# Splitting V into two float16 parts on ScalarE and VectorE in an attention + MoE kernel, with a new table of due times

## The chip, the cores and the metric

The kernel runs on one core of one Trainium2 chip, as one program. The time is the device time of the whole program in microseconds (us). An engine's name in the profile is PE for TensorE's matmuls, PEld for its weight loads, DVE for VectorE, ACT for ScalarE, POOL for GpSimd and SP for SyncE, which here only starts DMAs.

## The reference, cut to what matters

Attention with rotary position embedding, for 4 batches x 8 heads, 576 tokens, 64 elements to a head:

```python
q_rot, k_rot = (rotate(q), rotate(k))
scores = scale * np.matmul(q_rot, k_rot.transpose(0, 1, 3, 2))
scores = scores - np.max(scores, axis=-1, keepdims=True)
attn = np.exp(scores)
attn = attn / (np.sum(attn, axis=-1, keepdims=True) + 1e-09)
return np.matmul(attn, v)
```

Its output, as 2304 tokens of 512 elements, goes through a mixture of 8 experts: gate probabilities P are normalised over rows and columns in turn eight times, and the output is the sum over e of P[:, e] * (relu(x @ w1[e]) @ w2[e]), with 1024 hidden elements.

## The kernel before, in words

**Two parts of a number.** TensorE multiplies float16 here wherever it can. A float32 operand is scaled by a power of two and split into a high part, which is its float16 rounding, and a low part, which is the float16 rounding of what is left. A product is then three matmuls: high x high, high x low, low x high. V, the softmax weights, x and the expert weights are all split so. The scores (line 406) are float32 matmuls.

**Attention.** The 32 heads are worked as 16 pairs, two heads side by side on the 128 partitions. For a pair, GpSimd turns q and k (rope: four multiplications, line 357, and two additions, line 361), and TensorE makes five score groups of four matmul instructions each (S, line 406; the profile has eight records to a group, 640 for the 80 groups). Each row block of scores is a tile of PSUM, of which three stand at a time. Per tile: VectorE takes the row maximum (line 410), ScalarE the exponential (line 417), VectorE the reciprocal of the sum (lines 423 and 425), ScalarE writes the scaled high part (line 428), VectorE the low part (line 292). In four tiles of nine the exponential is written to an SBUF tile `e`, and the scores' PSUM tile is free from there on; in the other five it stays in PSUM tile `s` until the low part is made. SyncE then starts a transposing DMA of the two parts (lines 458 and 462) into ET. Once a half pair's transposes have landed, TensorE multiplies them with V's parts (AV, line 477), and ScalarE and VectorE split the result into `xx` (lines 487 and 489).

**V.** A batch's V is loaded in four pieces of 128x640 (line 318). VectorE takes the largest magnitude of each (line 289), then of the four (line 328); TensorE turns that column into a row and spreads the result back to all partitions (lines 660 and 667; the same helper serves the gate's weights and expert 0's weights), and VectorE makes a power of two of it (lines 279 to 285). Before the change, for each of the 16 pairs: GpSimd multiplies the piece by that power in place (`v_x`, line 384), ScalarE casts it to the high part (`v_hi`, line 379), and GpSimd subtracts (`v_lo`, line 388). Two tiles hold split V (NVV = 2).

**Expert 0 inside attention.** The weights of expert 0 are scaled and split in the same way, in place on GpSimd (`wz`, line 549), ScalarE (`wh`, line 545) and GpSimd (`wl`, line 553). As soon as x of a batch is there, TensorE may run expert 0's first product (F1, line 611) and, once the last of the second weight's low parts is there, its second (F2, line 630); the code asks for `wl.2.7`, the eighth and last `wl` of that weight. These matmuls fill TensorE between score groups. The gate's normalisation and experts 1 to 7 (line 1092, a seven-product scheme over half experts) follow.

**What sets the order.** Each engine runs its instructions in the order in which they were recorded. That order is made at build time by a list scheduler (`Plan.run`): every operation has an engine, a cost in us, a due time `at` and dependencies; at each step an idle engine takes the ready operation with the smallest due time. The due times of the attention part are `AT`, `AT_NEW` and the offsets `SH1`, one to a kind of operation: `S` scores, `M` maximum, `ex` exponential, `ei` reciprocal, `eh` and `el` high and low part, `TR` transposes, `AV`, `ld` and `ldv` loads, `cq sq aq` and `ck sk ak` rope of q and k, `vx vh vl` V's scaling, high and low part. `choice(...)` gives GpSimd alone here, because BOTH is False. `lock=True` tells the scheduler that a VectorE operation is not to be put beside a GpSimd operation.

Of the kernel before, what the change touches and what calls it, by code (L numbers as in the profile page):

```python
# [14 lines left out]
ALU = mybir.AluOpType  # L15
# [4 lines left out]
B, H, S, D = 4, 8, 576, 64  # L20
NT, DM, NE, DF = B * S, 512, 8, 1024
NPAIR = B * H // 2
KC = DM // P
# [39 lines left out]
    ld=-78.23, cq=-29.0, ck=-28.0, vx=-11.0, sq=-29.0, sk=-28.0, aq=-28.5, ak=-27.5, vh=-10.0, vl=-9.0, h0=4.69, l0=5.19,  # L63
    h1=9.69, l1=10.19, S=-20.0, M=-20.0, ex=-20.0, eh=-10.0, el=-10.0, TR=-10.0, AV=5.0, ei=-20.0,
)
AT_NEW = dict(ldv=-30.41, v0=-10.46, v1=-9.46, v2=-8.46, v3=-7.46, vg=-6.96, vr=-6.86, vp=-6.46)
AV_AT = ((3, 0, 0), (3, 0, 1), (4, 0, 2), (5, 0, 3), (6, 0, 4), (7, 1, 0), (8, 1, 1), (9, 1, 2), (10, 1, 3), (11, 1, 4))

SH1 = dict(
    cq=11.55, sq=11.55, aq=11.55, el=9.37, vh=-16.21, ld=10.14, M=-76.45, S=-26.64, eh=-9.66, ex=-20.25, ck=-11.34,  # L70
    sk=-11.34, ak=-11.34, ldv=-6.42, AV=-36.11, TR=10.32, vx=11.72, vl=-32.41, x0=1.13, h0=1.13, l0=1.13, x1=1.13,
    h1=1.13, l1=1.13, ei=-12.59,
)

US = dict(
# [147 lines left out]
def attention_moe(ctx, tc, qk, v, trigs, eye, wg, w1, w2, out):  # L223
# [67 lines left out]
    def stt_lo(lo, x, s, hi):  # L291
        dve.scalar_tensor_tensor(lo, x, s, hi, op0=ALU.mult, op1=ALU.subtract)  # L292

    def hi_of(hi, x, s, e="act"):
        if e == "act":
            act.activation(hi, x, AF.Copy, scale=s)
        else:
            dve.tensor_scalar(hi, x, s, None, op0=ALU.mult)
# [76 lines left out]
    def v_hi(p):  # L375
        t = att.tile([P, 2, 640], F16, tag="vv", bufs=NVV, name="vv")
        vhl[p] = [t[:, n].rearrange("p (j a d) -> p j a d", j=2, a=5) for n in range(2)]
        b, c = divmod(p, KC)
        act.copy(vhl[p][0], vraw[b][:, c])

    def v_x(p, e):
        b, c = divmod(p, KC)
        x = vraw[b][:, c].rearrange("p j a d -> p (j a d)")
        engine[e].tensor_scalar(x, x, vs[b], None, op0=ALU.mult)

    def v_lo(p, e):
        b, c = divmod(p, KC)
        engine[e].tensor_tensor(vhl[p][1], vraw[b][:, c], vhl[p][0], op=ALU.subtract)

    HEADS = [slice(0, 64), slice(64, P)]  # L390
    QH = [slice(0, HS), slice(HS, S)]
# [258 lines left out]
    def choice(pool_us, dve_us):  # L650
        return (("pool", US[pool_us]), ("none", 0.0))[:1] + ((("dve", US[dve_us]),) if BOTH else ())
# [25 lines left out]
    def pair_ops(p):  # L677
# [4 lines left out]
        def add(k, e, us, fn, deps=(), **kw):  # L682
            e = e if isinstance(e, tuple) else (e, US[us])
            plan.add(f"{k}.{p}", e, at[k], fn, [d if "." in d else f"{d}.{p}" for d in deps], **kw)
# [11 lines left out]
        for i in range(5):  # L696
# [14 lines left out]
            for j in range(1 if i == TAIL else 2):  # L711
# [19 lines left out]
                    f"TR.{m}", ("sp", US["TR"]), at["TR"] + u + off(u), lambda m=m: e_turn(m), [f"el.{m}"] + [f"et{h}.{p}" for h in hs],  # L731
                    uses=[e] + [(f"ET{h}", p) for h in hs], allocs=tails if u == 4 else [],
                )
        add("vx", choice("tsv", "tsd"), 0, lambda e: v_x(p, e), [f"vp.{b}"], uses=[("vraw", b)])
        add("vh", "act", "vh", lambda: v_hi(p), ["vx"], allocs=[("vhl", p)], uses=[("vraw", b)])
        add("vl", choice("plv", "tt"), 0, lambda e: v_lo(p, e), ["vh"], uses=[("vraw", b), ("vhl", p)])
        done = None
        for s, qh, jt in AV_AT:
            a, et = ("G", ("av", p, qh)), (f"ET{qh}", p)
# [63 lines left out]
    def w0_ops():  # L803
        plan.add("gx", ("dve", 0.3), 8, gate_max)
        last, g = top_ops("g", 8, "gx", lambda: w0m["g"])
        plan.add("gs", ("dve", 1.0), 8, gate_scale, [last], uses=[g], lock=True)
        for n, at in ((1, 16.95), (2, 66.94)):
            r = ("raw0", n)
            for i in range(4):
                plan.add(  # L810
                    f"w.{n}.{i}", ("sp", 5.5), at - 30 + 2 * i, lambda n=n, i=i: w0_load(n, i), [f"w.{n}.{i - 1}"] if i else [],
                    allocs=[] if i else [r], uses=[r] if i else [],
                )
                plan.add(f"wm.{n}.{i}", ("dve", US["w"]), at + i, lambda n=n, i=i: w0_max(n, i), [f"w.{n}.{i}"] + ([f"wm.{n}.{i - 1}"] if i else []), uses=[r])
            plan.add(f"wx.{n}", ("dve", 0.25), at + 4, lambda n=n: w0_max1(n), [f"wm.{n}.3"])
            last, g = top_ops(f"w{n}", at + 4, f"wx.{n}", lambda n=n: w0m[n])
            plan.add(f"ws.{n}", ("dve", 0.7), at + 5, lambda n=n: w0_scale(n), [last], uses=[g], lock=True)
            for i in range(8):
                d = [f"wz.{n}.{i - 1}"] if i else []
                plan.add(f"wz.{n}.{i}", choice("tsw", "tsd"), at + 5 + 3 * i, lambda e, n=n, i=i: w0_x(n, i, e), [f"ws.{n}"] + d, uses=[r])  # L820
                d = [f"wh.{n}.{i - 1}"] if i else []
                plan.add(f"wh.{n}.{i}", ("act", US["wh"]), at + 6 + 3 * i, lambda n=n, i=i: w0_hi(n, i), [f"wz.{n}.{i}"] + d, uses=[r])
                d = [f"wl.{n}.{i - 1}"] if i else []
                plan.add(f"wl.{n}.{i}", choice("plw", "wl"), at + 7 + 3 * i, lambda e, n=n, i=i: w0_lo(n, i, e), [f"wh.{n}.{i}"] + d, uses=[r])
        plan.add("acc", ("none", 0.0), 0, open_acc, ["wl.2.7"])
# [598 lines left out]
```

## Time and profile before

| | us |
|---|---|
| median of 3 runs | 1685.58 |
| lowest and highest run | 1684.28, 1691.61 |
| the profiled execution's own time | 1691.59 |
| its span, first to last instruction | 1689.6 |
| last attention matmul (line 477) starts | 425.7 |
| engines' busy share of the span: PE, DVE, ACT, POOL | 94%, 82%, 62%, 36% |

The profiled execution is near the slowest of the runs shown, 6.0 us above the median, of which 2.0 us lie outside the span. Attention takes the first quarter of the span, and the change lies in that quarter alone; the mean shares of the whole say little about it. The page's 40 slices (42.2 us each) show a PE that fills up only from the sixth slice on, and a granted clock below full in the slices before.

### The profile page before, as it was taken

The page shows a single profiled execution, that of the slowest core. Times are in us where ns is not written, and L with a number is a line of the kernel's source. Part 1 is how long each engine was busy: PE and PEld are TensorE (multiplying, and loading weights), DVE is VectorE, ACT ScalarE, POOL GpSimd, SP SyncE. Part 2 cuts the span into 40 slices and gives each one's busy share as a digit, 9 for nine tenths or more (in the row PEclk, how much of TensorE's full clock was granted, in tenths as well). Part 3 has the DMA queues.
Part 4 walks back from the last instruction along what each step waited for, and adds up shares of the span by engine and source line. Part 5 has one row for each costly group of instructions (what it writes and reads, how often), then busy time and mean ns, then how long its engine had stood idle before and what let it go on. Part 6 is the DMA issues. An engine that isn't in the chain of part 4 may idle for free.

```text
span 1689.6 us, 35290 instructions
## 1 busy us (share of the span) xinstructions
PE 1583.7 (94%) x13990; PEld 1274.3 (75%) x13990; DVE 1377.7 (82%) x2736; ACT 1054.4 (62%) x2145; POOL 616.1 (36%) x504
## 2 busy tenths in 40 slices
PE   3676889999998999999999999999999999999998
PEld 2343445445456898989989898989898989898987
DVE  7667977877797888888888888888888878888877
ACT  3565766656237666666666666666666666666642
POOL 4767774620252423232323323232323323333310
PEclk9767988999999999999999999999999999999999
DMA  7899989977122565656555565655555555565532
GB/s 215 176 184 189 213 177 188 190 155 125 54 88 100 125 151 125 151 132 157 125 151 136 140 138 143 157 131 146 138 151 138 143 133 155 126 161 130 127 111 94
DMA packets 244853, 243.61 MB, mean 144 GB/s; under 512 B 195792, under 2 KB 195920, under 8 KB 241104
## 3 DMA queue, kind: packets, MB, share of 16 engines
q1 hardware_dynamic: 225968, 180.02, 39.5%
q0 software_dynamic: 18720, 61.35, 20.3%
q8 instruction: 109, 1.79, 0.4%
q14 instruction: 56, 0.46, 0.1%
HBM read 123.36 MB, written 9.44 MB: 79 GB/s over the span
## 4 chain that ended last, share of the span: by engine, by line
PE 79%; DVE 8%; DMA 3%; ACT 2%; issue 2%; SPq 0%; POOLq 0%; ACTq 0%; DVEq 0%
PE m L1092 66%; PE s L406 4%; PE g L477 4%; DMA ET<-et 3%; PE g L630 3%; PE g L611 2%; DVE et L292 2%; DVE nm L410 1%; DVE hl L621 1%; DVE ts L912 0%; ACT accA L879 0%; ACT et L428 0%; ACT e L417 0%; DVE w1l L292 0%; DVE ei L425 0%
## 5 line engine op out<-in xcount | busy, mean ns | idle before, releaser
L1092 PE MATMUL m<-w2h,h 128*128 128x256 f16 x3528 | 627.2, 273 | 3.2 <-DVE accB L1155 1.5
L1092 PEld LDWEIGHTS <-h 128*128 128x128 f16 x5292 | 515.3, 98 | 63.5 <-issue 2.0
L1092 PE MATMUL m<-w2l,h 128*128 128x256 f16 x1764 | 480.8, 273 | 0.0
L1092 PEld LDWEIGHTS <-w1h 128*128 128x128 f16 x3920 | 369.2, 98 | 39.9 <-issue 3.0
L1092 PE MATMUL m<-ts,w1h 128*128 128x256 f16 (+1 forms) x2240 | 347.6, 262 | 2.7 <-ACT m L1115 1.4
L1157 ACT ACTIVATE ev<-m,pp 128x256 f32<-128x256 f32 x468 | 197.6, 467 | 185.8 <-PE m L1092 184.8
L1092 PE MATMUL m<-ts,w1l 128*128 128x256 f16 (+1 forms) x1120 | 284.0, 262 | 0.0
L1092 PE MATMUL m<-xx,w1h 128*128 128x256 f16 (+1 forms) x1680 | 261.4, 262 | 0.0
L1042 POOL TENSOR_TENSOR wraw<-wraw 128x512 f32<-128x512 f32 x112 | 160.8, 1436 | 169.3 <-issue 140.6
L1092 PE MATMUL m<-xx,w1l 128*128 128x256 f16 (+1 forms) x840 | 213.1, 262 | 0.0
L1137 POOL TENSOR_TENSOR h<-u,h 128x512 f16<-128x512 f32 (+1 forms) x70 | 78.2, 1116 | 357.7 <-ACT h L1133 348.8
L1092 PEld LDWEIGHTS <-w1l 128*128 128x128 f16 x1960 | 191.8, 98 | 17.7
L1155 DVE SCALAR_TENSOR_TENSOR ev<-m,pp,ev 128x256 f32<-128x256 f32 x351 | 154.8, 478 | 45.4 <-ACT ev L1157 28.3
L406 PE MATMUL s<-raw 64*128 64x288 f32 (+1 forms) x640 | 136.7, 509 | 49.7 <-ACT e L417 19.5
L1133 ACT ACTIVATE h<-m 128x512 f16<-128x512 f32 (+1 forms) x210 | 120.4, 574 | 44.4 <-PE m L1092 40.8
L406 PEld LDWEIGHTS s<-raw 64*128 64x128 f32 (+1 forms) x640 | 72.2, 211 | 99.8 <-issue 28.0
L410 DVE TENSOR_REDUCE nm<-s 128x1 f32<-128x576 f32 x144 | 103.6, 752 | 48.6 <-PE s L406 48.1
L1118 DVE TENSOR_TENSOR u<-m,u 128x512 f32<-128x512 f32 (+1 forms) x140 | 88.9, 635 | 54.9 <-PE m L1092 29.2
L1133 ACT ACTIVATE h<-u 128x512 f16<-128x512 f32 (+1 forms) x210 | 122.4, 586 | 14.8 <-DVE u L1144 11.1
L1115 ACT COPY u<-m 128x512 f32<-128x512 f32 (+1 forms) x140 | 75.8, 541 | 71.5 <-PE m L1092 70.4
L1165 POOL DMA_DIRECT2D accA<-ev x78 | 69.0, 1021 | 126.5 <-ACT ev L1157 108.4
L1165 POOL DMA_DIRECT2D accB<-ev x52 | 45.1, 867 | 181.7 <-ACT h L1133 111.0
(148 smaller groups left out, 2629.8 us busy)
## 6 DMA issues: line engine op xcount, KB each, us to landing
ts<-xd SPq DMA_DIRECT2D x110, 512.0 KB, 3.8
accA<-ev POOLq DMA_DIRECT2D x78, 512.0 KB, 6.1
wraw<-in_w SPq DMA_DIRECT2D x28, 1024.0 KB, 4.9
raw<-in_qk SPq DMA_DIRECT2D x32, 576.0 KB, 5.0
accB<-ev POOLq DMA_DIRECT2D x26, 512.0 KB, 7.1
ts<-xd SPq DMA_DIRECT2D x28, 256.0 KB, 2.9
accB<-ev POOLq DMA_DIRECT2D x26, 256.0 KB, 3.3
vraw<-in_v SPq DMA_DIRECT2D x16, 320.0 KB, 4.4
```

The costliest lines, as they stand in the source:

```text
L406: pe.matmul(o, q, x[r, 1, QH[kh]], start=True, stop=True)
L410: dve.tensor_reduce(b[0], ps[:, :, 0:HS], axis=AX.XY, op=ALU.max, negate=True)
L477: pe.matmul(po[r, m : m + e.shape[-1]], x[:, j, jt, :], e[:, j, 5 * n + jt, :], start=jt == i == 0 and x is vh and n == 0, stop=jt == 4 an ...
L1042: put(k, "pool", US["ptt"], lambda: pool.tensor_tensor(quad(o), quad(x), quad(y), op=op), deps, uses=[raw])
L1092: pe.matmul(live[bank][:, f_ * width : (f_ + 1) * width], step(x, i, f_), y[:, i], start=first and f_ == 0 and n == 0, stop=n == 5, skip_g ...
L1115: act.copy(live[n], live[src])
L1118: dve.tensor_tensor(live[n], live[x], live[n], **add)
L1133: act.activation(t[:, 0:cols], live[src], func)
L1137: engine[eng].tensor_tensor(l, live[src], h, **sub)
L1155: dve.scalar_tensor_tensor(o, x, s, o, op0=ALU.mult, op1=ALU.add)
L1157: act.activation(o, x, AF.Copy, scale=s)
L1165: pool.dma_start(out=accs(th * NT2 + t0_, nt), in_=ev[th][:, 0:nt], accum_op=ALU.add)
```

## The change

V's high part is now made from the raw piece by one ScalarE activation with the power of two as its scale, and its low part by one VectorE instruction, raw x scale - high (`stt_lo`). The multiplication in place on GpSimd is gone, and so is GpSimd's subtraction. The operation count of V goes from three to two per pair. The due times are a new set: `AT_NEW` for V's maximum and scale, all of `SH1`, and the due times of expert 0's two weights. The instructions of the gate's part and of experts 1 to 7 stand in the same order as before on every engine; VectorE's last 2039 instructions and TensorE's last 23493 are the same.

```diff
-AT_NEW = dict(ldv=-30.41, v0=-10.46, v1=-9.46, v2=-8.46, v3=-7.46, vg=-6.96, vr=-6.86, vp=-6.46)
+AT_NEW = dict(ldv=-30.41, v0=-12.6, v1=-11.6, v2=-10.6, v3=-9.6, vg=-9.1, vr=-9.0, vp=-8.6)
 SH1 = dict(
-    cq=11.55, sq=11.55, aq=11.55, el=9.37, vh=-16.21, ld=10.14, M=-76.45, S=-26.64, eh=-9.66, ex=-20.25, ck=-11.34,
+    cq=-15.86, sq=-15.86, aq=-15.86, el=6.56, vh=-15.55, ld=29.61, M=-83.32, S=-99.0, eh=-8.21, ex=-31.64, ck=-3.35,
...
-        act.copy(vhl[p][0], vraw[b][:, c])
-
-    def v_x(p, e):
-        b, c = divmod(p, KC)
-        x = vraw[b][:, c].rearrange("p j a d -> p (j a d)")
-        engine[e].tensor_scalar(x, x, vs[b], None, op0=ALU.mult)
+        hi_of(vhl[p][0], vraw[b][:, c], vs[b])
 
-    def v_lo(p, e):
+    def v_lo(p):
         b, c = divmod(p, KC)
-        engine[e].tensor_tensor(vhl[p][1], vraw[b][:, c], vhl[p][0], op=ALU.subtract)
+        stt_lo(vhl[p][1], vraw[b][:, c], vs[b], vhl[p][0])
...
-        add("vx", choice("tsv", "tsd"), 0, lambda e: v_x(p, e), [f"vp.{b}"], uses=[("vraw", b)])
-        add("vh", "act", "vh", lambda: v_hi(p), ["vx"], allocs=[("vhl", p)], uses=[("vraw", b)])
-        add("vl", choice("plv", "tt"), 0, lambda e: v_lo(p, e), ["vh"], uses=[("vraw", b), ("vhl", p)])
+        add("vh", "act", "vh", lambda: v_hi(p), [f"vp.{b}"], allocs=[("vhl", p)], uses=[("vraw", b)])
+        add("vl", "dve", "vl", lambda: v_lo(p), ["vh"], uses=[("vraw", b), ("vhl", p)], lock=True)
...
-        for n, at in ((1, 16.95), (2, 66.94)):
+        for n, at in ((1, 17.16), (2, 58.97)):
```

The functions that it calls stood there before:

```python
def stt_lo(lo, x, s, hi):
    dve.scalar_tensor_tensor(lo, x, s, hi, op0=ALU.mult, op1=ALU.subtract)

def hi_of(hi, x, s, e="act"):
    if e == "act":
        act.activation(hi, x, AF.Copy, scale=s)
```

In the changed kernel the lines from `v_hi` on stand five lines earlier and those after the pair's operations six. Three places show what the new due times do.

VectorE, early in the program, up to the maximum over batch 0's V (`vm1`); `vmx` is the maximum of a piece of V, `wmx` of a quarter of expert 0's first weight, `wgs` the split gate weights, `nm` the row maximum of scores. Before:

```order
L279 TENSOR_SCALAR e_285<-g_165 128x1
L283 TENSOR_SCALAR inv_287<-e_285 128x1
L285 RECIPROCAL s_289<-inv_287 128x1
L588 TENSOR_SCALAR wgs_94<-wgt_93,s_289 128x4x8
L589 SCALAR_TENSOR_TENSOR wgs_94<-wgt_93,s_289,wgs_94 128x4x8
L289 TENSOR_REDUCE wmx_213<-wraw_149 128x1
L289 TENSOR_REDUCE vmx_195<-vraw_142 128x1
L328 TENSOR_REDUCE vm1_299<-vmx_195 128x1
```

And now:

```order
L289 TENSOR_REDUCE wmx_211<-wraw_149 128x1
L405 TENSOR_REDUCE nm_267<-s_258 128x1
L405 TENSOR_REDUCE nm_270<-s_259 128x1
L289 TENSOR_REDUCE vmx_191<-vraw_142 128x1
L418 TENSOR_SCALAR et_280<-es_272 128x1
L420 RECIPROCAL ei_282<-et_280 128x1
L418 TENSOR_SCALAR et_284<-es_278 128x1
L420 RECIPROCAL ei_286<-et_284 128x1
L289 TENSOR_REDUCE wmx_211<-wraw_149 128x1
L289 TENSOR_REDUCE vmx_191<-vraw_142 128x1
L328 TENSOR_REDUCE vm1_297<-vmx_191 128x1
```

The gate weights' five small instructions no longer stand ahead of `vm1`; a third `wmx` does.

TensorE at the same moment: the two matmuls that spread V's maximum (L660 and L667 before, L655 and L662 now), between score groups. Before:

```order
L406 MATMUL s<-raw 128x288 x8
L660 LDWEIGHTS vm_299
L660 MATMUL g<-idt,vm_299 1x128
L667 LDWEIGHTS neg
L667 MATMUL g<-top_309,neg 128x1
L406 MATMUL s<-raw 128x288 x8
```

And now:

```order
L401 MATMUL s<-raw 128x288 x8
L655 LDWEIGHTS vm_297
L655 MATMUL g<-idt,vm_297 1x128
L401 MATMUL s<-raw 128x288 x4
L662 LDWEIGHTS neg
L662 MATMUL g<-top_311,neg 128x1
L401 MATMUL s<-raw 128x288 x4
```

The sixth score group has moved between the two, so that it no longer stands behind the second.

GpSimd, where expert 0's second weight is finished (`wraw` scaled, `wl` its low parts) beside the rope of two pairs. Before, `raw_1848` is pair 9's and `raw_2085` pair 10's:

```order
L549 TENSOR_SCALAR wraw_1285<-wraw_1285,s_1724 128x512
L357 TENSOR_TENSOR raw_1848<-raw_1848,trig_95 128x576
L357 TENSOR_TENSOR raw_1849<-raw_1849,trig_95 128x576
L361 TENSOR_TENSOR raw_1848<-raw_1848,raw_1849 128x576
L357 TENSOR_TENSOR raw_1848<-raw_1848,trigq_96 128x576
L357 TENSOR_TENSOR raw_1849<-raw_1849,trigq_96 128x576
L361 TENSOR_TENSOR raw_1848<-raw_1848,raw_1849 128x576
L553 TENSOR_TENSOR wl_1727<-wraw_1285,wh_1726 128x512 x3
L549 TENSOR_SCALAR wraw_1285<-wraw_1285,s_1724 128x512 x2
L553 TENSOR_TENSOR wl_1727<-wraw_1285,wh_1726 128x512 x2
L357 TENSOR_TENSOR raw_2085<-raw_2085,trig_95 128x576
```

And now, where `raw_2056` is pair 10's:

```order
L548 TENSOR_TENSOR wl_1794<-wraw_1041,wh_1793 128x512
L357 TENSOR_TENSOR raw_2056<-raw_2056,trigq_96 128x576
L357 TENSOR_TENSOR raw_2057<-raw_2057,trigq_96 128x576
L361 TENSOR_TENSOR raw_2056<-raw_2056,raw_2057 128x576
L357 TENSOR_TENSOR raw_2056<-raw_2056,trig_95 128x576
L357 TENSOR_TENSOR raw_2057<-raw_2057,trig_95 128x576
L361 TENSOR_TENSOR raw_2056<-raw_2056,raw_2057 128x576
L548 TENSOR_TENSOR wl_1794<-wraw_1041,wh_1793 128x512 x2
L544 TENSOR_SCALAR wraw_1041<-wraw_1041,s_1791 128x512 x2
L548 TENSOR_TENSOR wl_1794<-wraw_1041,wh_1793 128x512 x2
```

The last four `wl` now stand behind the rope of pair 10, one pair later than before. On TensorE the first F2 matmul stands behind 46 score groups instead of 41, the first F1 matmul behind 24 instead of 28. Counted at the end of score group 46, 135 matmuls of expert 0 stood ahead before and 96 now; at group 58, 222 and 231; at the last group, 438 and 432.

## Rows read from the trace of the kernel before

**Rows 1.** The page: busy time by engine, and the clock in 40 slices.

```profile
PE 1583.7 (94%) x13990; PEld 1274.3 (75%) x13990; DVE 1377.7 (82%) x2736; ACT 1054.4 (62%) x2145; POOL 616.1 (36%) x504
...
PEclk9767988999999999999999999999999999999999
```

**Rows 2.** Busy us by stretch (window, length, engines), then granted clock, DMA share, GB/s.

```profile
40.00:165.00 125.00, 84.56 (x527) 50.47 (x528) 89.54 (x200) 73.74 (x155) 92.11 (x62) 0.76 0.90 184
165.00:205.00 40.00, 36.26 (x250) 18.52 (x246) 35.40 (x79) 28.75 (x61) 26.43 (x19) 0.99 0.96 211
205.00:235.00 30.00, 20.44 (x114) 12.15 (x115) 22.40 (x49) 17.91 (x39) 25.37 (x18) 0.66 0.94 193
235.00:440.00 205.00, 192.80 (x1486) 102.87 (x1486) 154.24 (x348) 129.09 (x269) 78.28 (x56) 0.97 0.79 156
440.00:522.00 82.00, 77.10 (x410) 40.11 (x408) 74.98 (x141) 30.96 (x56) 35.17 (x24) 1.00 0.21 76
```

**Rows 3.** The page: the chain that ended last, shares of the span by line.

```profile
PE m L1092 66%; PE s L406 4%; PE g L477 4%; DMA ET<-et 3%; PE g L630 3%; PE g L611 2%; DVE et L292 2%; DVE nm L410 1%; DVE hl L621 1%; DVE ts L912 0%; ACT accA L879 0%; ACT et L428 0%; ACT e L417 0%; DVE w1l L292 0%; DVE ei L425 0%
```

**Rows 4.** The score matmuls alone, line 406, by stretch: PE, PEld, clock, DMA.

```profile
40.00:160.00 120.00, 47.87 (x184) 25.36 (x184) 0.76 0.89 182
160.00:240.00 80.00, 24.38 (x120) 12.55 (x120) 0.85 0.91 194
240.00:320.00 80.00, 25.48 (x144) 14.21 (x144) 0.94 1.00 203
320.00:400.00 80.00, 22.40 (x136) 11.60 (x136) 0.98 0.76 141
```

**Rows 5.** What TensorE waited for in 0 to 240 us: total us, times, longest.

```profile
PE s L406 <- ACT e L417: 17.8, 13, 2.9
PE g L477 <- DMA ET<-et: 17.3, 8, 5.4
PE s L406 <- DVE et L292: 13.3, 7, 4.9
PE g L660 <- DVE vm L328: 11.1, 2, 8.7
PE s L406 <- POOL vv L388: 1.8, 1, 1.8
```

**Rows 6.** Groups by form in 0 to 440 us: busy us, mean ns, idle before.

```profile
L292 DVE SCALAR_TENSOR_TENSOR et<-e,ei,et 128x576 f16<-128x576 f32 x64 | 66.1, 1032 | 0.9 <-ACT et L428 0.8
L292 DVE SCALAR_TENSOR_TENSOR et<-s,ei,et 128x576 f16<-128x576 f32 x80 | 64.6, 810 | 15.0 <-ACT et L428 14.7
L428 ACT ACTIVATE et<-e,ei 128x576 f16<-128x576 f32 x64 | 49.5, 773 | 6.6 <-issue 2.6 <-ACT s L417 1.2 <-ACT xx L487 0.6
L384 POOL TENSOR_SCALAR vraw<-vraw,s 128x640 f32<-128x640 f32 x16 | 31.5, 1975 | 2.0 <-DVE s L285 2.0
L388 POOL TENSOR_TENSOR vv<-vraw,vv 128x640 f16<-128x640 f32 x16 | 22.4, 1397 | 68.8 <-ACT vv L379 68.8
L379 ACT CAST vv<-vraw 128x640 f16<-128x640 f32 x16 | 11.6, 723 | 9.2 <-PE g L477 9.2
```

**Rows 7.** Line 292 in 0 to 440 us: shortest, median, longest ns; first and last start.

```profile
L292 DVE SCALAR_TENSOR_TENSOR et<-e,ei,et x64: 796/819/1982, 28.5 to 413.3; 128x576 f16<-128x576 f32 x64
```

**Rows 8.** The timeline of DVE and PE around 36 to 41 us: start, length, what.

```profile
36.01 1.45 DVE L589 SCALAR_TENSOR_TENSOR wgs<-wgt,s,wgs 128x32 f16<-128x32 f32 x1
37.38 1.21 DVE L289 TENSOR_REDUCE wmx<-wraw 128x1 f32<-128x1024 f32 x1
39.34 0.16 DVE L328 TENSOR_REDUCE vm<-vmx 128x1 bf16<-128x4 f32 x1
39.56 0.27 PE L660 MATMUL g<-idt,vm 128*1 128x128 bf16 x1 [8.72 <-DVE vm L328]
...
40.87 0.16 PE L667 MATMUL g<-top,neg 1*128 1x1 bf16 x1 [1.04 <-DMA ET<-et]
```

**Rows 9.** The timeline of POOL around 223 us, as the second weight's low parts end.

```profile
223.15 2.62 POOL L553 TENSOR_TENSOR wl<-wraw,wh 128x512 f16<-128x512 f32 x2 [4.40 <-ACT wh L545]
225.73 3.27 POOL L357 TENSOR_TENSOR raw<-raw,trig 128x576 f32<-128x576 f32 x2
...
235.02 1.40 POOL L361 TENSOR_TENSOR raw<-raw 128x576 f32<-128x576 f32 x1
```

**Rows 10.** The F2 matmuls alone, line 630, by stretch: PE, PEld, clock, DMA.

```profile
360.00:400.00 40.00, 14.81 (x63) 5.58 (x63) 1.00 0.71 128
```

More of the change, by code (lines that the diff above doesn't have):

```diff
@@ L65 @@
 )
-AT_NEW = dict(ldv=-30.41, v0=-10.46, v1=-9.46, v2=-8.46, v3=-7.46, vg=-6.96, vr=-6.86, vp=-6.46)
+AT_NEW = dict(ldv=-30.41, v0=-12.6, v1=-11.6, v2=-10.6, v3=-9.6, vg=-9.1, vr=-9.0, vp=-8.6)
 AV_AT = ((3, 0, 0), (3, 0, 1), (4, 0, 2), (5, 0, 3), (6, 0, 4), (7, 1, 0), (8, 1, 1), (9, 1, 2), (10, 1, 3), (11, 1, 4))
 SH1 = dict(
-    cq=11.55, sq=11.55, aq=11.55, el=9.37, vh=-16.21, ld=10.14, M=-76.45, S=-26.64, eh=-9.66, ex=-20.25, ck=-11.34,
-    sk=-11.34, ak=-11.34, ldv=-6.42, AV=-36.11, TR=10.32, vx=11.72, vl=-32.41, x0=1.13, h0=1.13, l0=1.13, x1=1.13,
-    h1=1.13, l1=1.13, ei=-12.59,
+    cq=-15.86, sq=-15.86, aq=-15.86, el=6.56, vh=-15.55, ld=29.61, M=-83.32, S=-99.0, eh=-8.21, ex=-31.64, ck=-3.35,
+    sk=-3.35, ak=-3.35, ldv=3.34, AV=-35.53, TR=50.6, vx=12.14, vl=-38.21, x0=-3.51, h0=-3.51, l0=-3.51, x1=-3.51,
+    h1=-3.51, l1=-3.51, ei=9.58,
 )
```

## The prediction

> **What bounds the kernel now.** The page comes first: PE is busy 94% of the span, and its clock falls below full only in the first slices [rows 1]. So I cut the span by stage [rows 2]. From 440 us on, and in all of experts 1 to 7, the change moves nothing; there the chain of waits is TensorE's own matmuls, 66% of it on line 1092 alone [rows 3]. From 235 to 440 us PE is busy 192.8 of 205 us at a clock of 0.97: TensorE bounds that stretch as well, because expert 0's matmuls fill it. Before 235 us nothing is full: in 40 to 165 us PE is busy 84.6 of 125 us at a mean clock of 0.76 (a mix of its two levels, 1.2 and 2.4 GHz), VectorE 89.5, ScalarE 73.7, GpSimd 92.1, the DMA engines 0.90 [rows 2]. That is a pipeline held by its latencies. Its pace is read from the score matmuls, eight records to a group [rows 4]: 184 records are 23 groups in 120 us, 5.2 us each; then 15 in 80 us, 5.3 each; then, with more of expert 0 between them, 18 in 80 us (4.4) and 17 in 80 us (4.7). What TensorE waits for up to 240 us is ScalarE's exponential 17.8 us, the transposing DMAs 17.3, VectorE's low parts 13.3, V's maximum 11.1 and GpSimd's V 1.8 [rows 5]. The question is what the change does to the first 235 us, and whether TensorE then has the same work left.
>
> **The change, part by part.** All terms are us on the path; negative is a gain.
>
> GpSimd's V work. 16 multiplications (31.5) and 16 subtractions (22.4) go, 53.9 us of GpSimd [rows 6], 24% of the 222.2 that it is busy from 40 to 440 us [rows 2]. Only what TensorE waited for counts: 1.8 [rows 5]. Term -1.8; from -1.8 to 0.
>
> ScalarE's high part. 16 casts of 723 ns become scaled activations. The scaled copy of 128x576 out of SBUF takes 773 ns [rows 6], so 859 ns for 640 columns: 16 x 0.136 = 2.2 us more. ScalarE is busy 59% of 40 to 165 us [rows 2], which hides it. Term 0; up to 2.2 without that cover.
>
> VectorE's low part. 16 new instructions, a form that the trace has from SBUF with 576 columns: shortest 796, longest 1982 ns [rows 7], mean 1032 [rows 6]. By columns (640 to 576) that is 0.88 to 2.2 us each; I take the mean, 1.15, the nearest row. Against it, the same instruction with its large operand in PSUM takes 810 ns [rows 6], so the 64 from SBUF spend 66.1 - 64 x 0.810 = 14.3 us in waits, which I put down to GpSimd; 24% less GpSimd work saves 3.4 of them. Eight of the 16 low parts fall ahead of 235 us, as eight pairs' V does before: 8 x 1.15 - 1.7 = 7.5 us more on VectorE there. The other eight lie beside a full TensorE. VectorE idles 28% of 40 to 165 us, and what stands behind a low part is a row maximum or a reciprocal, for which ScalarE's exponential and then the next score group wait. I take a third of it on the path: +2.5; from -1.7 (they fill idle time, the savings do not) to 7.5.
>
> For this price the row shows a median of 819 ns against a longest of 1982 [rows 7], so most of the 64 met nothing. The Trainium skill, "SBUF — State Buffer", section "Who interferes with whom", says that a VectorE instruction with two SBUF inputs and a GpSimd instruction that reads SBUF shut each other out for a whole instruction; the new low part has two such inputs and the old VectorE share of V had none. Were each of the first eight shut out for one GpSimd subtraction of 1.4 us [rows 6], that would be an estimate of 11.2 us of VectorE time instead of the 2.2 that the mean holds above the shortest, and the term +5.5 instead of +2.5.
>
> The first V maximum. TensorE stood 8.7 us for it, until 39.56, and began group 6 only behind the second matmul of that helper, at 40.97 [rows 8]. On VectorE the gate weights' last instruction goes from ahead of it (36.01 to 37.38: -1.4) and a third maximum over a weight comes in (37.38 to the next start, at most 1.21: +1.2); on TensorE group 6 now follows the first helper matmul at once (39.83 instead of about 41.0: -1.2). Term -1.4; from -2.6 to 0.
>
> Expert 0's second product. It may begin once the last `wl` is through, which was at 225.8 [rows 9], and that now stands behind the rope of pair 10, which ran from 225.73 until 236.4, one V multiplication among it [rows 9]. In order, the first F2 matmul comes five score groups later, and 39 matmuls that stood ahead of the end of group 46 stand behind it: at 14.81/63 = 0.235 us [rows 10] 9.2 us of TensorE work leave a stretch with idle TensorE for one that is 94% full. The 24 F1 matmuls that now stand four groups earlier go the other way, but they lay in latency-bound time before and still do. By group 58 the order has caught up (231 against 222), so part of the 39 goes into idle time of 235 to 280 us. I take half: +4.6; from 0 to 9.2.
>
> The rest of the new order. Half-pair products stand up to three score groups earlier, maxima and low parts change places everywhere. The order does not say what that is worth. It can touch the three waits of 17.8, 17.3 and 13.3, 48.4 us together [rows 5]: I bound it by a quarter of them either way, 12, and take a tenth as a gain, -5, since GpSimd's rope, which feeds the scores, now runs without V's work between.
>
> Sum: -1.8 + 0 + 2.5 - 1.4 + 4.6 - 5 = -1.1. On the profiled execution's own 1691.59 that is 1690.5; this execution lies 6.0 above the median of the runs, 1685.58, so the forecast for the median is 1684.5: no change.
>
> **The rivals.** 0.5% of the time is 8.4 us; that is about what a measurement of this kernel can tell from none.
>
> Faster: the first 235 us become denser. For it speak 48.4 us of waits that depend on order [rows 5], a TensorE that in 40 to 165 us is busy 68% at 0.76 of its clock, and a later pace of 4.4 to 4.7 us with the same softmax work per group [rows 4]. Against it: the DMA engines are at 0.89 to 1.00 from 40 to 320 us [rows 4]. If the 38 groups of 40 to 240 us go at 4.85 instead of 5.2 to 5.3, 38 x 0.4 = 15 us are won: 1670. Chance 0.28.
>
> Slower: TensorE runs dry before expert 0's second product. Between the end of the first F1 block and the first F2 matmul stand 13 score groups now. Before, the dry stretch of 205 to 235 us shows what that costs: PE busy 20.4 of 30 us at a clock of 0.66 [rows 2]. If groups 42 to 46 go at 5.3 instead of 4.4 (4.5 us) and the 39 matmuls find no idle TensorE later (9.2), 13.7 us are lost; with the other terms, which sum to -5.7 without this one, and the reordering's -5 not coming, 1685.6 + 13.7 - 0.7 = 1698.6. It decides when the 12 us that PE idles from 235 to 440 us [rows 2] are no room for late matmuls. The Trainium skill, "TensorE: Matmul & The Clock Gate", Part 1, says that the clock is granted by how busy the array was kept; the trace agrees (0.66 where PE was busy 68%, 0.99 where 91%) [rows 2], and by that rule the dry stretch pays twice. Chance 0.23.
>
> The transfers set the pace: at 0.98 and more they would be the bound, whatever the engines do, and GpSimd's relief shows only as idle time. For it: a share of 1.00 in 240 to 320 us [rows 4]. Against it: the same share goes with 4.4 us a group there and 0.89 with 5.2 before. That gives 1685.6, within no change.
>
> **How the numbers follow.** No change, the transfers' case in it, has 0.49, with a range of its own of 1677.2 to 1694.0 (the median and 8.4 either way); faster 0.28, slower 0.23. The known ends, -1.8 + 0 - 1.7 - 2.6 + 0 - 12 = -18.1 and 0 + 2.2 + 7.5 + 0 + 9.2 + 12 = 30.9, do not fall together; from them and the rivals' 1670 and 1698.6 I take 1667 to 1701 for 8 times in 10.
>
> **What would show it.** GpSimd's busy time in 40 to 440 us some 54 us lower; 16 new VectorE instructions of 128x640 at a mean near 1.15 us; group 6 beginning within 0.3 us of the first V maximum's matmul; the first F2 matmul 5 groups later, at about 240 us or after, with a clock near 0.7 in the 30 us before; PE busy over 90% from 250 us on; the last attention matmul within 8 us of 425.7. I am wrong if the pace of 40 to 160 us leaves 5.0 to 5.4 us a group, if VectorE's new instructions cost under 0.9 or over 1.5 us, or if expert 1's first matmul moves while the last attention matmul does not.

## The result, and the profile after

The changed kernel takes 1669.46 us, median of 4 runs (1666.99 to 1673.73), beside 1688.59 (4 runs) for the kernel before, timed with it: ratio 0.9885, 95% interval 0.9859 to 0.9912, 19 us faster. The forecast of 1684.5, no change, was wrong; the time lies in its range near the low end, at the figure of the rival that I called faster (1670). The profiled execution took 1673.73 us, its span 1672.0, 17.6 less than the span before; it is the slowest of its four, as the profile before is near the slowest of its own.

Busy time by stretch in the changed kernel (window, length, then PE, PEld, DVE, ACT, POOL, granted clock, DMA share, GB/s):

```profile
40.00:165.00 125.00, 94.91 (x635) 55.61 (x636) 106.82 (x234) 82.98 (x174) 69.04 (x48) 0.82 1.02 205
165.00:205.00 40.00, 31.83 (x197) 17.36 (x193) 31.78 (x73) 27.69 (x57) 29.03 (x21) 0.83 0.90 185
205.00:235.00 30.00, 18.96 (x142) 12.54 (x144) 24.25 (x58) 21.70 (x46) 16.75 (x13) 0.62 0.98 182
235.00:440.00 205.00, 196.66 (x1482) 104.04 (x1479) 161.47 (x372) 125.21 (x256) 54.90 (x42) 0.99 0.75 149
440.00:522.00 82.00, 75.83 (x455) 44.27 (x453) 68.36 (x115) 42.98 (x79) 35.18 (x24) 1.00 0.27 93
```

Against [rows 2], 40 to 165 us is denser on every engine but GpSimd: VectorE 106.8 us busy instead of 89.5, PE 94.9 instead of 84.6, while GpSimd falls from 92.1 to 69.0. The score matmuls alone, line 401 now (PE, PEld, clock, DMA):

```profile
40.00:160.00 120.00, 44.71 (x193) 22.74 (x192) 0.83 1.02 203
160.00:240.00 80.00, 31.49 (x128) 15.97 (x128) 0.72 0.96 196
240.00:320.00 80.00, 23.00 (x144) 12.31 (x144) 1.00 0.92 184
320.00:400.00 80.00, 20.39 (x132) 10.70 (x128) 1.00 0.80 146
```

From 40 to 240 us 321 records are 40.1 groups, where [rows 4] had 304, or 38: 5.0 us each instead of 5.3. Counting groups by their records' starts, eight to a group, shows when the lead over the kernel before arises (us, at the start of the group; the kernel before's start stands in the heading, and the kernels below the first row are the experiments' further down):

| kernel | 34 (191.0) | 43 (235.0) | 46 (247.9) | 58 (302.7) | 67 (351.6) | 80 (407.8) |
|---|---|---|---|---|---|---|
| changed | 16.6 | 15.1 | 10.0 | 10.0 | 18.2 | 17.1 |
| new_ops_old_table | 10.5 | 1.5 | 0.0 | -1.3 | 4.9 | 2.3 |
| old_ops_new_table | 9.2 | 9.3 | 10.1 | 6.1 | 13.0 | 10.2 |
| gp_busy | 14.6 | 11.9 | 7.2 | 2.5 | 10.3 | 9.9 |
| w2_early30 | 19.4 | 18.7 | 16.1 | 11.8 | 17.0 | 13.5 |
| f2_two | 18.1 | 17.9 | 12.5 | 14.3 | 23.4 | 17.2 |

The changed kernel is 15.1 us ahead by 235 us, falls back to 10.0 in the stretch ahead of its late F2, and has it all again by group 67. What TensorE waited for in 0 to 240 us (total us, times, longest):

```profile
PE g L472 <- DMA ET<-et: 22.9, 13, 5.5
...
PE s L401 <- ACT e L412: 11.1, 10, 2.6
PE s L401 <- DVE et L292: 10.6, 9, 1.8
PE g L655 <- DVE vm L328: 6.0, 2, 4.2
```

The three long waits of [rows 5] together hardly fell, from 48.4 to 44.6 us; V's maximum fell by 5.1, and GpSimd's V is gone. The instructions of the new V path and the low parts of the softmax in 0 to 440 us (busy us, mean ns, idle before):

```profile
L292 DVE SCALAR_TENSOR_TENSOR et<-e,ei,et 128x576 f16<-128x576 f32 x64 | 65.0, 1016 | 1.2 <-ACT et L423 1.2
L292 DVE SCALAR_TENSOR_TENSOR et<-s,ei,et 128x576 f16<-128x576 f32 x80 | 64.3, 808 | 6.0 <-ACT et L423 5.6
...
L292 DVE SCALAR_TENSOR_TENSOR vv<-vraw,s,vv 128x640 f16<-128x640 f32 x16 | 14.9, 930 | 1.3 <-ACT vv L296 1.3
L296 ACT ACTIVATE vv<-vraw,s 128x640 f16<-128x640 f32 x16 | 13.0, 822 | 5.7 <-PE g L472 5.7
```

And the first V maximum, from the timeline of the changed kernel around 36 us:

```profile
36.41 0.16 DVE L328 TENSOR_REDUCE vm<-vmx 128x1 bf16<-128x4 f32 x1
...
36.62 0.27 PE L655 MATMUL g<-idt,vm 128*1 128x128 bf16 x1 [4.24 <-DVE vm L328]
36.82 0.85 PE L401 MATMUL s<-raw 64*128 64x288 f32 x1
```

It comes 2.9 us earlier than in [rows 8], and group 6 follows at once, 4.2 us earlier. All of the 17.6 us of the profiles is there when attention ends. The attention matmuls and expert 1's first matmuls, first of the kernel before, then of the changed one (shortest, median, longest ns; first and last start):

```profile
L477 PE MATMUL g<-ET,vv x960: 269/286/449, 51.8 to 425.7; 128*64 128x288 f16 x168, 128*64 128x256 f16 x24
...
L1092 PE MATMUL m<-xx,w1h x1680: 219/272/273, 521.3 to 1673.1; 128*128 128x256 f16 x147, 128*128 128x128 f16 x40
```

```profile
L472 PE MATMUL g<-ET,vv x960: 276/286/450, 43.8 to 408.1; 128*64 128x288 f16 x168, 128*64 128x256 f16 x24
...
L1086 PE MATMUL m<-xx,w1h x1680: 219/272/273, 504.5 to 1655.4; 128*128 128x256 f16 x147, 128*128 128x128 f16 x40
```

The last attention matmul starts 17.6 us earlier, and from it to the end of the span it is 1263.9 us in both (1689.6 - 425.7 and 1672.0 - 408.1). The page's chain reads as [rows 3] did: 67% on expert matmuls.

### The profile page after: what moved, and what is told of

Read it like the earlier page. It is cut to its first block, busy times and chain, and to the rows that moved or that the text cites. A ratio compares the mean times of both kernels' runs of the same rounds, so it can differ in the third digit from the quotient of the medians.

```text
span 1672.0 us, 35276 instructions
## 1 busy us (share of the span) xinstructions
PE 1580.0 (95%) x13990; PEld 1273.2 (76%) x13990; DVE 1386.2 (83%) x2752; ACT 1056.5 (63%) x2145; POOL 563.5 (34%) x472
## 4 chain that ended last, share of the span: by engine, by line
PE 78%; DVE 6%; ACT 2%; DMA 2%; issue 2%; SPq 0%; POOLq 0%; ACTq 0%; DVEq 0%
PE m L1086 67%; PE g L625 3%; PE g L472 3%; PE g L606 2%; PE s L401 2%; DMA ET<-et 2%; DVE et L292 1%; DVE nm L405 1%; DVE ts L906 0%; ACT accA L873 0%; DVE hl L616 0%; DVE w1l L292 0%; DVE u L921 0%; DVE u L931 0%; ACT et L423 0%
## 5 line engine op out<-in xcount | busy, mean ns | idle before, releaser
L401 PE MATMUL s<-raw 64*128 64x288 f32 (+1 forms) x640 | 137.7, 496 | 37.5 <-ACT e L412 12.4
L1127 ACT ACTIVATE h<-u 128x512 f16<-128x512 f32 (+1 forms) x210 | 122.3, 586 | 14.8 <-DVE u L1138 11.1
L472 PE MATMUL g<-ET,vv 128*64 128x288 f16 (+1 forms) x960 | 85.9, 326 | 30.5 <-DMA ET<-et 27.4
```

Of the source, the lines that this page charges most:

```text
L401: pe.matmul(o, q, x[r, 1, QH[kh]], start=True, stop=True)
L472: pe.matmul(po[r, m : m + e.shape[-1]], x[:, j, jt, :], e[:, j, 5 * n + jt, :], start=jt == i == 0 and x is vh and n == 0, stop=jt == 4 an ...
L1127: act.activation(t[:, 0:cols], live[src], func)
```

## The experiments

Each ratio is to the kernel before as it was timed beside that run (medians of 1686.05 to 1688.90), so ratios compare better than medians do. "Left" is how many of expert 0's 432 F2 matmuls begin after the last attention matmul, "rest" the span less that matmul's start, both in the profiled execution.

| kernel | ratio to before, interval | median us | last attention matmul | rest | first F2 | left |
|---|---|---|---|---|---|---|
| before | | 1688.59 | 425.7 | 1263.9 | 224.9 | 240 |
| changed | 0.9885 [0.9859, 0.9912] | 1669.46 | 408.1 | 1263.9 | 239.7 | 240 |
| new_ops_old_table | 0.9988 [0.9973, 1.0002] | 1684.60 | 421.9 | 1264.5 | 238.3 | 204 |
| old_ops_new_table | 1.0155 [1.0129, 1.0180] | 1715.56 | 413.8 | 1291.7 | 298.9 | 249 |
| gp_busy | 0.9946 [0.9925, 0.9968] | 1679.25 | 415.4 | 1263.9 | 242.8 | 240 |
| w2_early30 | 0.9956 [0.9939, 0.9973] | 1680.63 | 410.8 | 1267.5 | 221.5 | 210 |
| f2_two | 0.9893 [0.9868, 0.9918] | 1669.48 | 407.3 | 1261.6 | 236.7 | 160 of 288 |
| sink4 | 0.9879 [0.9861, 0.9898] | 1668.53 | 409.2 | 1260.3 | 240.2 | 240 |
| both_light | 0.9868 [0.9842, 0.9894] | 1666.08 | 405.8 | 1258.5 | 238.6 | 160 of 288 |
| recip_back | 1.0021 [1.0007, 1.0035] | 1691.39 | 424.2 | 1264.6 | 237.7 | 195 |
| vmax_back | 0.9935 [0.9913, 0.9957] | 1675.99 | 413.7 | 1263.0 | 210.0 | 177 |
| xhalf_back | 1.0021 [1.0006, 1.0035] | 1690.77 | 418.2 | 1269.8 | 234.3 | 240 |
| old_ei_x | 0.9955 [0.9938, 0.9972] | 1682.74 | 413.6 | 1263.2 | 214.5 | 177 |
| old_ei_x_v | 0.9961 [0.9947, 0.9975] | 1682.97 | 417.8 | 1264.2 | 232.8 | 240 |

**The two halves of the change.** new_ops_old_table has the new operations under the old table:

```diff
-AT_NEW = dict(ldv=-30.41, v0=-12.6, ...
+AT_NEW = dict(ldv=-30.41, v0=-10.46, ...
-    cq=-15.86, ... S=-99.0, ... ei=9.58,      (all of SH1)
+    cq=11.55, ... S=-26.64, ... ei=-12.59,
-        for n, at in ((1, 17.16), (2, 58.97)):
+        for n, at in ((1, 16.95), (2, 66.94)):
```

> The changed kernel's operations for V with the due times of before (AT_NEW, SH1 and the two weights' times). Theory A (the operations themselves: V's split is shorter and GpSimd is relieved, so the first half-pair product starts some 8 us earlier and the pipeline stays ahead by that): most of the gain is here, 1668 to 1676 us, the first product at line 472 near 44 us. Theory B (the new due times make the gain, the operations alone none): 1682 to 1690 us, ratio to before 0.997 to 1.003.

old_ops_new_table is the reverse: the kernel before with these three edits made the other way.

> The operations of before (GpSimd multiplies in place and subtracts) with the new due times. Theory A: no gain or a loss, 1685 to 1700 us, since this table was fitted to other operations and the first product still waits for GpSimd, near 50 us. Theory B: 1668 to 1676 us.

Neither half wins in time: 0.9988, which is no change, as theory B had it, and 1.0155, slower than either theory allowed (its profiled execution, 1707.54 us, is the fastest of its five). Together they give 0.9885. But at the last attention matmul they nearly add: the operations alone are 3.8 us ahead of the kernel before, the table alone 11.9, both 17.6. What ruins the table with the old operations lies behind attention, where its rest is 27.8 us longer. GpSimd, with V's old work in its queue, ends the last `wl` at 295.1 us instead of 240.1 in the changed kernel; F2 begins at 298.9, and 537 of expert 0's matmuls (288 F1, 249 F2) are left behind the last attention matmul instead of 432 (192 and 240). From that matmul to expert 1's first, in the kernel before and then in old_ops_new_table:

```profile
425.70:521.30 95.60, 90.52 (x516) 46.47 (x512) 85.21 (x162) 33.92 (x63) 42.59 (x32) 1.00 0.21 75
```

```profile
413.80:537.20 123.40, 113.36 (x624) 56.86 (x619) 94.05 (x170) 38.76 (x72) 42.96 (x32) 1.00 0.19 69
```

22.8 us more of TensorE stand beside 27.8 us more of time, so late matmuls are the likely price here; it is argued, for no run moved `wl` alone under these operations. With the new operations alone TensorE still stood for the first V maximum as it did before (line 655, 0 to 60 us):

```profile
PE g L655 <- DVE vm L328: 8.2, 1, 8.2
```

**GpSimd's work given back.** gp_busy is the changed kernel with a multiplication and a subtraction on each piece of V behind its low part, on GpSimd, whose results nobody reads; the rest of the order is kept:

```diff
         stt_lo(vhl[p][1], vraw[b][:, c], vs[b], vhl[p][0])
+        x = vraw[b][:, c].rearrange("p j a d -> p (j a d)")
+        pool.tensor_scalar(x, x, vs[b], None, op0=ALU.mult)
+        pool.tensor_tensor(x, x, x, op=ALU.subtract)
```

> The changed kernel, every engine in its order, but behind each low part of V GpSimd does a multiplication and a subtraction of the same 128x640 piece again, whose results nothing reads: its 54 us of V work are back, V's shorter path stays. If the gain is GpSimd's relief (fewer waits of VectorE, rope earlier): 1680 to 1690 us. If it is V's shorter path and the order: 1668 to 1674 us, with the low parts of the softmax (line 292 out of SBUF) back at a mean near 1.03 us.

Its 1679.25 us lie between the two ranges. It gives back 0.0061 of the ratio, 10 us of the 19, and 7.3 us of the 17.6 at the last attention matmul. Its GpSimd groups and VectorE's low parts, in 0 to 440 us (busy us, mean ns, idle before):

```profile
L292 DVE SCALAR_TENSOR_TENSOR et<-e,ei,et 128x576 f16<-128x576 f32 x64 | 62.6, 980 | 1.2 <-ACT et L426 1.2
...
L385 POOL TENSOR_SCALAR vraw<-vraw,s 128x640 f32<-128x640 f32 x16 | 31.4, 1961 | 79.5 <-DVE vv L292 49.9 <-DVE et L421 18.8 <-ACT s L415 6.8
...
L386 POOL TENSOR_TENSOR vraw<-vraw 128x640 f32<-128x640 f32 x16 | 20.6, 1286 | 1.3
...
L292 DVE SCALAR_TENSOR_TENSOR vv<-vraw,s,vv 128x640 f16<-128x640 f32 x16 | 15.8, 991 | 1.3 <-ACT vv L296 1.3
```

52 us of GpSimd are back, yet the softmax's low parts are no longer for it (980 ns against 1016) and V's only by 61 ns each: longer VectorE instructions are not the way the 7 us are lost. What the rows do show is where GpSimd stood: its added multiplications waited 79.5 us for others, above all for V's low part on VectorE, with the rope of the next pairs queued behind them in order. GpSimd's last rope instruction ends at 347.9 us, in the changed kernel at 341.4. That order, not contention, is the likely way. So the 7 to 10 us are the price of this work with these waits; a run that separates the two was not made.

**An earlier second product.** In w2_early30 the scaling and parts of expert 0's second weight are due 30 us earlier:

```diff
+                at2 = at - (30 if n == 2 else 0)
-                plan.add(f"wz.{n}.{i}", choice("tsw", "tsd"), at + 5 + 3 * i, ...
+                plan.add(f"wz.{n}.{i}", choice("tsw", "tsd"), at2 + 5 + 3 * i, ...
...
```

> The changed kernel with the due times of expert 0's second weight's scaling and parts 30 us earlier, so that all eight low parts stand ahead of pair 10's rope and the first F2 matmul behind 43 score groups instead of 46. If a late F2 costs what the prediction took for it (4.6 of at most 9.2 us): 1663 to 1667 us, and the lead over before is held through groups 45 to 65 instead of shrinking from 17 to 9 us. If that shrinking has another cause, or late matmuls find idle time anyway: 1668 to 1672 us.

F2 began 18 us earlier, at 221.5, and the kernel became 11 us slower, outside both ranges. Up to group 52 the first theory was right: the lead stands at 16.1 us at group 46 and 17.4 at group 52, where the changed kernel has 10.0 and 12.8. It is lost later, 10.7 against 12.4 at group 64 and 13.5 against 17.1 at group 80, and the rest is 3.6 us longer. The edit reorders every engine, so what costs the 11 us stays open; an earlier F2 gained nothing in this order.

**Which entry of the table.** recip_back, vmax_back and xhalf_back put one entry of the changed kernel back:

```diff
-    ... ei=9.58,
+    ... ei=-12.59,          (recip_back)
-    x0=-3.51, h0=-3.51, l0=-3.51, x1=-3.51, h1=-3.51, l1=-3.51
+    x0=1.13, h0=1.13, l0=1.13, x1=1.13, h1=1.13, l1=1.13          (xhalf_back)
-v0=-12.6, v1=-11.6, v2=-10.6, v3=-9.6, vg=-9.1, vr=-9.0, vp=-8.6
+v0=-10.46, v1=-9.46, v2=-8.46, v3=-7.46, vg=-6.96, vr=-6.86, vp=-6.46          (vmax_back)
```

> Changed kernel with one due time of the new table back at its old value: that of the softmax reciprocal (ei -12.59 instead of 9.58), so that VectorE takes a ready reciprocal before other ready work instead of after it. Theory (the table wins as a whole because it was fitted to the new operations, no single entry carries it): a part of the 19 us is lost, 1672-1682 (0.990 to 0.996). Rival one (this entry carries the gain): 1683-1692 (0.997 or more), first attention product and pace of the score groups as with the old table. Rival two (it carries nothing): 1666-1672.

> Changed kernel with the due times of the attention output's halves (x, high and low parts) back at their old values, 4.64 us later, so that VectorE takes them after other ready work more often. Theory (no single entry carries it): 1670-1682 (0.989 to 0.996). Rival one (it carries the gain): 1683 or more (0.997 or more). Rival two (nothing): 1666-1672.

> Changed kernel with the due times of V's maximum (loading of V unchanged) back at their old values, 2.14 us later. Theory (no single entry carries it): first attention matmul later than 43.8 by 2 to 8 us, and half of that or less left at the end of attention: 1670-1680 (0.989 to 0.995). Rival (the earlier start of V's path is the gain, since the first attention product started 8 us earlier and the lead was 10 us at group 12): last attention matmul 8 us or more later, 1677-1690 (0.993 to 1.001).

Two entries each took the whole gain away and the third 0.5% of the 1.15%, so they cannot be shares of a sum. My theory gave each a part only; vmax_back's time fell in its range, but its first attention matmul did not move (43.7 us), where I had expected 2 to 8 us. With the reciprocal's old time the first V maximum is late again (TensorE's waits, 0 to 60 us):

```profile
PE g L655 <- DVE vm L328: 7.9, 1, 7.9
```

With V's own old times the wait was 4.2 us as in the changed kernel: the earlier V maximum comes from letting reciprocals wait on VectorE, not from V's due times. In recip_back's timeline the gate weights' five instructions (33.23 to 35.75) stand ahead of `vm1` again; in vmax_back they do not. The reverse test puts new entries into new_ops_old_table, first two, then three:

```diff
-    ... x0=1.13, h0=1.13, l0=1.13, x1=1.13, h1=1.13, l1=1.13, ei=-12.59,
+    ... x0=-3.51, h0=-3.51, l0=-3.51, x1=-3.51, h1=-3.51, l1=-3.51, ei=9.58,          (old_ei_x, old_ei_x_v)
-AT_NEW = dict(ldv=-30.41, v0=-10.46, ...
+AT_NEW = dict(ldv=-30.41, v0=-12.6, ...          (old_ei_x_v)
```

> Changed operations with the old table, in which two entries have their new values: the softmax reciprocal (ei 9.58) and the halves of the attention output (-3.51), the two whose return to the old value took the whole gain away. Theory (these two carry the gain together): 1668-1676 (0.988 to 0.993). Rival (the gain belongs to the whole order, and each entry matters only beside all the others): 1678-1700 (0.994 or more).

> As the run with two new entries in the old table, and with V's maximum due 2.14 us earlier as a third. Theory (the three carry the gain): 1666-1673 (0.987 to 0.991). Rival (the whole order): 1676-1700 (0.993 or more).

0.9955 and 0.9961: a third of the gain, and the third entry adds nothing. My theory that these entries carry it fell. Each entry moves hundreds of instructions behind it, and of the tables tried only the whole one has the gain.

**What sets the time behind attention.** f2_two leaves out a third of expert 0's second product, 144 matmuls (34 us at the 0.235 us of [rows 10]). sink4 leaves out four of eight normalisation rounds of the gates (32 VectorE instructions, about 10 us). both_light leaves out both.

```diff
-        for n, (a, x) in enumerate(((hh, wh), (hh, wl), (hl, wh))):
+        for n, (a, x) in enumerate(((hh, wh), (hh, wl))):          (f2_two, both_light)
-        for _ in range(SINK):
+        for it in range(SINK):          (sink4, both_light)
+            if it >= 4:
+                yield
+                yield
+                yield
+                continue
```

> Left out: the third of expert 0's second product that multiplies the low part of the hidden values, 144 of its 432 matmuls, some 34 us of TensorE work at 0.235 us each, from 240 us to the end of expert 0. Theory (the end is set by the last attention product and a chain behind it that VectorE leads): attention ends at most 8 us earlier than 408.1, the stretch from the last attention matmul to expert 1's first matmul stays at 88 to 97 us, and the time falls by 0 to 15 us, to 1655-1669 (ratio to the kernel before 0.980 to 0.989). Rival (the prediction's premise: TensorE is full from 235 us on and every matmul taken out counts): about 30 us less, 1635-1645 (0.968 to 0.974).

> Left out: the last four of the eight rounds of row and column normalisation of the gates, 32 VectorE instructions (about 10 us of VectorE at 2.5 us a round) and 4 small matmuls behind the last attention product; the rest stays in its order. Theory (behind the last attention matmul VectorE's chain sets the end of the stage): the stretch from the last attention matmul (408) to expert 1's first matmul is 86 to 91 us instead of 96, the time 1659-1664 (ratio to the kernel before 0.983 to 0.986). Rival (TensorE, which is over 90% busy there, sets it): stretch unchanged, 1668-1671 (0.988 to 0.990).

> Left out: both what f2_two leaves out (144 matmuls of expert 0's second product) and what sink4 leaves out (four of eight normalisation rounds of the gates, about 10 us of VectorE). Each alone shortened the stretch from the last attention matmul to expert 1's first matmul by some 3 us (96.4 to 93.3 and 92.9). Theory (TensorE and VectorE are both full there, so relief of one leaves the other): the stretch falls to 82-89 us, the time to 1657-1665 (ratio to the kernel before 0.982 to 0.987). Rival (a chain of weights, their sums on GpSimd and the x sums sets it, whichever engine is relieved): 90-93 us, 1665-1669 (0.987 to 0.989).

The windows 240 to 410 and 410 to 500 us of the changed kernel, then of f2_two, sink4 (second window) and both_light (second window), with columns as above:

```profile
240.00:410.00 170.00, 163.44 (x1283) 86.35 (x1282) 135.82 (x301) 115.74 (x237) 45.55 (x34) 1.00 0.85 163
410.00:500.00 90.00, 84.94 (x476) 43.65 (x473) 81.10 (x157) 32.32 (x60) 40.59 (x32) 1.00 0.18 65
```

```profile
240.00:410.00 170.00, 156.21 (x1236) 83.92 (x1234) 130.96 (x296) 113.20 (x233) 45.94 (x33) 0.97 0.86 162
410.00:500.00 90.00, 74.79 (x374) 37.61 (x373) 84.59 (x160) 33.10 (x62) 41.26 (x30) 0.94 0.20 73
```

```profile
410.00:500.00 90.00, 87.14 (x494) 44.43 (x492) 74.97 (x128) 33.43 (x62) 43.34 (x32) 1.00 0.21 76
```

```profile
410.00:500.00 90.00, 76.74 (x398) 39.92 (x398) 75.23 (x124) 36.77 (x70) 41.30 (x29) 0.94 0.23 82
```

34 us less TensorE work moved neither the time (ratio 0.9893 against 0.9885, intervals overlapping) nor the last attention matmul (407.3 against 408.1): PE's busy share fell, and the rest is 2.3 us shorter. That refutes the premise that every matmul taken out from 235 us on counts. But not all of the relief became idle time. In 240 to 410 us 70 fewer F2 matmuls (16.5 us at 0.235) lowered PE's busy time by 7.2 us only, since the granted clock fell to 0.97. f2_two was 5.2 us ahead of the changed kernel at group 68 (331.1 against 336.3); then TensorE stood for 3.0 us, at the last for a transposing DMA, and the block of V's matmuls behind it ran at a granted clock of 0.50, the lower of its two levels, in the changed kernel at 1.00. First f2_two, then the changed kernel (start, length, what):

```profile
335.59 3.81 PE L472 MATMUL g<-ET,vv 128*64 128x288 f16 x29 [1.44 <-DMA ET<-et]
```

```profile
339.36 2.02 PE L472 MATMUL g<-ET,vv 128*64 128x288 f16 x29 [1.19 <-DMA ET<-et]
```

By group 72 the lead was gone (356.9 against 357.0). How much of it the lower clock ate, and how much waits would have taken at full clock, no run shows. My next theory, VectorE's chain, predicted 1659 to 1664 for sink4 and missed too: the stretch from the last attention matmul to expert 1's first fell from 96.4 to 92.9 us, the median by 1 us, within the intervals. With both lighter that stretch was 90.2 us, the time 1666.08, as the rival had it, though 90.2 is close to the theory's 89. So neither TensorE's nor VectorE's amount of work alone sets that stretch, and less of it shortens the rest by 2 to 5 us in single executions. The rest is 1263.0 to 1264.6 us in eight of the fourteen kernels of the table, whether 177 or 240 F2 matmuls are left; the others have 1258.5 to 1269.8, and old_ops_new_table, with 105 more matmuls of expert 0 left, 1291.7. vmax_back shows how it stays where fewer are left: expert 1 starts at 498.4, 6.1 us earlier than in the changed kernel, and then TensorE waits for VectorE's and ScalarE's results (TensorE's waits, 495 to 700 us):

```profile
PE m L1086 <- ACT m L1109: 5.1, 1, 5.1
PE m L1086 <- DVE ts L906: 4.3, 1, 4.3
```

Line 906 is the low part of expert 1's x sums, whose work, like the loading of its weights, may begin only when attention's last output is written (`rel.0`). That chain, spread over VectorE, ScalarE, GpSimd and a load, is what I take to be the bound; that it is this chain is argued from these waits, and no run shortened it by itself.

## Why the prediction was wrong, step by step

**The bound.** Right for 40 to 235 us: a pipeline held by latencies, and a denser one is faster. Wrong for 235 to 440 us, the step on which the rest was built: a TensorE that is busy 94% there is not the bound at this amount of work, for 34 us less of it gained nothing measurable (f2_two). With 105 matmuls more behind attention it likely is (old_ops_new_table). In the kernel before and the changed one the end is the last attention matmul plus 1263.9 us, so here every us won in attention counts in full.

**GpSimd's V work, -1.8.** Mis-sized. It fell by 52.5 us in 40 to 440 us, as expected, but given back at the new order it costs 7 to 10 us (gp_busy), with no wait of TensorE's matmuls for GpSimd's V in either run. My term counted only the wait in which GpSimd was the last link; what waits behind its queue shows under other names. The second weight's low parts are such a queue: with the new table they end 55 us later when GpSimd has V's old work to do.

**ScalarE's high part, 0.** Right: 822 ns each (859 expected), no wait for it on TensorE's list.

**VectorE's low part, +2.5.** The size was high: 930 ns (1150 expected), longest 1576. It costs nothing that shows: with the old table the new operations end attention 3.8 us earlier and change the time by -0.1%. Of the Trainium skill's rule on shared ports ("SBUF — State Buffer", "Who interferes with whom") the trace shows little at this place, because the two rarely meet: 13 of the 16 overlap no GpSimd instruction in time and take 865 to 886 ns, the three that do took 886, 1029 and 1576. So the +5.5, for which each of the first eight had to be shut out, did not come. The softmax's 64 agree with the rule: 36 without a GpSimd instruction beside them took 818 ns at most, the 28 with one 1283 on average. Nor did the saving of 3.4 us that I had put on GpSimd's account: the softmax's 64 low parts went from 66.1 to 65.0 us [rows 6].

**The first V maximum, -1.4.** Right in direction; group 6 came 4.2 us earlier. TensorE's share of it is the 1.2 us expected; `vm1` itself came 2.9 us earlier, not 0.2. All five of the gate weights' instructions (34.85 to 37.38 us before) left the place ahead of it, and I had taken off only the last. The first score group also began 1.0 us earlier, and the longest of the low parts ahead of `vm1` had taken 1.89 us before.

**Expert 0's second product, +4.6.** This step failed. F2 began 14.8 us later, at 239.7, with a clock of 0.62 in the 30 us before, all as the prediction's signs had it. The lead fell too, from 15.1 us at group 43 to 10.0 at group 46, near the 4.5 that the slower rival gave this stretch. But that did not last: it is 18.2 us at group 67, and 240 F2 matmuls are left behind attention in both kernels, so at the end the term is worth nothing. The 39 matmuls found room in 235 to 410 us. With it falls the slower rival here, whose condition (no room for late matmuls) did not hold; in old_ops_new_table, with F2 at 298.9, 105 more matmuls were left over, and the time was 1715.56.

**The rest of the new order, -5, 12 either way.** The term that decided, and it was sized too small. Between new_ops_old_table and the changed kernel the last attention matmul moves by 13.8 us, beyond my bound, and between the old operations under the two tables by 11.9. I had bounded it by a quarter of three waits; from the kernel before to the changed one these fell by 3.8 in all, so they were the wrong quantity to bound it by. VectorE's busy time in 40 to 165 us rose by 17 us, of which the new low parts are 6.3 (seven of them): that its idle time, 28% of that stretch, was what a better order used is a reading of these rows that no run tests.

**The rivals.** Faster came, by the mechanism named (denser first 235 us) and with its size: 15.1 us of lead by 235 us, where I had given it 15. The pace was 5.0 us a group instead of 4.85; the earlier group 6 made up the difference. Of my signs of being wrong the pace came, barely: 193 records in 40 to 160 us are 4.97 us a group, below the 5.0 to 5.4 of no change. That the range held the time is owed to this rival, to which I gave 0.28, not to the forecast. Transfers did not set the pace before: the DMA share rose from 0.90 to 1.02 in 40 to 165 us, 205 GB/s instead of 184. Whether they set it now is open, since the transposing DMAs are the longest of TensorE's waits (22.9 us, 17.3 before).

What stays open: why single entries of the table take the whole gain with them, and by which of its queues, rope or expert 0's second weight, GpSimd's relief reaches the end.

## What to carry to other kernels

Find the point whose distance to the end of the program stays the same from kernel to kernel, here the last attention matmul, price edits by what they do to it, and look for the edit at which the distance gives way; work on an engine that is 94% busy elsewhere may be free up to there. Take a lead stage by stage too: two halves that seem not to add in time did add at that point. A wait list shows only the last link: for an engine with 1.8 us on it, work given back cost 7 to 10, and taking a quarter of its work away frees whatever stands behind it. Price a refitted order together with its operations, by idle time of the engines it reorders, with a wide range to both sides: one entry put back took all of the gain.

## What was not expected of the hardware

TensorE's busy share is a weak sign of a bound: 163 of 170 us busy in 240 to 410 us, and 15 us of matmuls (64 of 0.235) taken out ahead of the last attention matmul left it within 0.8 us. Part of such relief goes to a lower granted clock: the same 29 matmuls took 3.81 us instead of 2.02. VectorE's scaled multiply-and-subtract out of SBUF was seldom lengthened: 930 ns on average beside 865 at the shortest, and 991 when GpSimd had 52 us more to do; every one over 900 ns overlapped a GpSimd instruction.
